# Selection matmuls replaced by VectorE lane shuffles in a fused hash-attention and gated-MLP kernel

## Chip, cores, metric

One core of one Trainium2 chip. The metric is device time in microseconds (us) of one execution of the whole kernel. Times of fast runs are compared with fast runs of the kernel before, taken in the same rounds on the same chip. A ratio is the mean time of one kernel's fast runs over the mean of the other's in the same rounds, so it is not quite the ratio of the medians that are quoted. All runs of this study were in the fast state. Executions of one kernel still spread over 1 to 5 us here, which will matter.

## The reference

Two stages. First, attention in which a query sees only the keys with the same hash: six random projections of each token, taken as sign bits. Then a gated MLP on the heads put side by side.

```python
q_bits = (q @ proj > 0); k_bits = (k @ proj > 0)          # 6 bits a token
mask = bucket(q_bits)[:, :, :, None] == bucket(k_bits)[:, :, None, :]
scores = where(mask, q @ k.T / 8, -1e9)                   # B=4, H=8, S=768, D=64
x = softmax(scores) @ v                                   # -> (3072, 512)
g = x @ w_gate; val = x @ w_val                           # 512 -> 1536
out = x + sigmoid(x @ w_res) * ((gelu(g) * val) @ w_out)  # 1536 -> 512
```

The kernel gets the mask out of the score matmul itself: beside the 64 rows of q and k it has 7 more, six bits as plus or minus a half and one level. A pair of tokens with unequal bits then gets a score so low that its exponential is nothing.

## The kernel before

Two heads make a pair; four batches have four pairs each, 0 to 15. A pair takes nine slots (the first one twelve) of one score chunk each, and a hand-written table says which other work is issued in which slot. The projection of batch b-1 is cut into single matmuls and dealt out into the slots of batch b, by estimated costs, so that TensorE never runs dry. Between two batches stand gate and value matmuls with nothing beside them.

How the bits come about: the hash matmul gives, for four quarters of the tokens (two heads or two pairs, q and k), 32 lanes each on its own 32 partitions; VectorE compares with zero ("hb"). A token's column is there, but four tokens of a stripe are stacked in lanes: lane 6a+i of a quarter is bit i of stripe a. Before the change, four matmuls with a selection table put the stripes side by side:

```python
def hash_half(p, dh, bank=(tp_ps, "tp")):
    ...
        nc.vector.tensor_scalar(hb, hs, 0.0, 0.5, op0=ALU.is_gt, op1=ALU.subtract)
        bits[p] = (hb, bit_pool.tile([P, n, P], BF16, tag="bits", name="bits"))

def spread_matmuls(p, dst, c0, c1):
    for c in range(c0, c1, 4):
        n = min(4, c1 - c)
        for a in range(4):
            nc.tensor.matmul(dst[:, c - c0:c - c0 + n, 32 * a:32 * a + 32],
                             sels[quarters(p)[1]][:, a].rearrange("p j n -> p (j n)"),
                             bits[p][0][:, c:c + n, :], start=True, stop=True)

def spread(p, c0, c1, bank=(tp_ps, "tp")):
    sp = bank[0].tile([P, c1 - c0, P], FP32, tag=bank[1], name="spr")
    spread_matmuls(p, sp, c0, c1)
    nc.vector.tensor_copy(bits[p][1][:, c0:c1, :], sp)      # PSUM -> SBUF

def mask_rows(p, engines=(nc.sync, nc.sync)):               # 7 rows into q's and k's tiles, by DMA
    for h in (1, 0):
        for side in range(2):
            ...
            engines[side].dma_start(mask_target(p, side, h), src[0:NROW])
```

And the table of the later groups, two pairs at a time (s0 is the first slot of pair p-2, so slot 18 is the first of pair p):

```python
for p in range(6, NPAIR, 2):
    ...
    for dh in range(2):
        at(s0 + 7 + dh, hash_half, p, dh)
    for i, s in enumerate((9, 12, 13)):
        at(s0 + s, spread, p, 4 * i, 4 * i + 4)
    at(s0 + 13, mask_rows, p)
    ...
    at(s0 + 10, load, p + 1, (2,))
    if p + 2 < NPAIR:
        at(s0 + 5, load, p + 2, (0, 1))
        at(s0 + 8, load, p + 3, (0, 1))
        at(s0 + 15, load, p + 2, (2,))
```

## Time and profile before

| | before |
|---|---|
| median time | 353.75 us (353.47 to 354.38, 4 runs) |
| span of the profiled run | 352.0 us |
| TensorE busy | 340.3 us, 97% |
| VectorE busy | 152.7 us, 43% |
| selection matmuls | 112, of which 96 are concerned |

In the views, PE is TensorE, PEld its weight loads, DVE VectorE, ACT ScalarE, POOL GpSimd, and SPq the queue in which SyncE issues transfers one after the other. PSUM is the memory that matmuls write to, in banks; "the chain" is the work that ended last, followed back step by step to what released it.

The page, the chain and the matmuls' start times are shown in the prediction. One view more is the backbone of what follows: the stretches between landmarks. I cut the span at the first gate matmul of each batch and at the first projection matmul after it. Here are the four attention stages of the kernel before. Columns: stretch, its length, then busy time and (instructions) of TensorE, its weight loads, VectorE, ScalarE and GpSimd, the granted clock, the share of the DMA engines, GB/s.

```profile
13.00:52.87 39.87, 36.65 (x514) 23.90 (x520) 23.35 (x40) 34.60 (x38) 31.25 (x44) 1.00 0.73 205
85.12:135.99 50.87, 49.84 (x525) 29.10 (x533) 24.77 (x37) 40.54 (x44) 33.78 (x40) 1.00 0.58 158
168.11:218.01 49.90, 49.41 (x524) 28.99 (x532) 22.56 (x34) 40.22 (x43) 31.15 (x36) 1.00 0.41 114
250.30:296.24 45.94, 45.18 (x472) 26.69 (x478) 15.62 (x26) 37.05 (x40) 16.32 (x17) 1.00 0.16 45
```

The second number of each line is the one to compare: how long the stage lasted.

### The profile page before, as it was taken

The numbers are of one execution on the slowest core, as the hardware profiler recorded it, in microseconds if no ns is written. First come the engines' busy times: TensorE is split into PE (matmuls) and PEld (weight loads), VectorE is DVE, ScalarE is ACT, GpSimd is POOL, SyncE is SP. The second block draws the span as 40 slices with busy tenths as digits, with TensorE's granted clock in tenths as the row PEclk, the third lists the DMA queues.
The fourth block names the chain that finished last, engine by engine and source line by source line (L and its number), as shares of the span: only waits on it lengthen the run. The fifth ranks groups of instructions, "written<-read, shape, count | busy, mean of one in ns | idle before, by whom it ended". The sixth has DMA issues, their size and how long they took to land.

```text
span 352.0 us, 7561 instructions
## 1 busy us (share of the span) xinstructions
PE 340.3 (97%) x3056; PEld 202.4 (57%) x3106; DVE 152.7 (43%) x231; ACT 211.3 (60%) x238; POOL 154.0 (44%) x194
## 2 busy tenths in 40 slices
PE   8999889999999999999999999999999999999995
PEld 4656466665565566656465566666555665666443
DVE  6975532435436427343344446333452024433343
ACT  5899895235787886323888788323778884232220
POOL 5798947675488487200068678400038222000000
PEclk9999999999999999999999999999999999999999
DMA  7875879998813882820005663510002221000012
GB/s 222 258 238 108 257 252 299 361 336 176 259 49 93 203 252 69 210 102 0 2 35 128 175 204 105 125 41 1 0 2 63 85 54 50 10 2 1 32 60 89
DMA packets 52718, 44.06 MB, mean 125 GB/s; under 512 B 31656, under 2 KB 44620, under 8 KB 52684
## 3 DMA queue, kind: packets, MB, share of 16 engines
q1 hardware_dynamic: 52540, 43.56, 42.6%
q8 instruction: 24, 0.39, 0.5%
q14 instruction: 10, 0.08, 0.1%
q0 software_dynamic: 64, 0.02, 0.0%
q10 hardware_dynamic: 80, 0.00, 0.0%
HBM read 29.36 MB, written 6.29 MB: 101 GB/s over the span
## 4 chain that ended last, share of the span: by engine, by line
PE 89%; ACT 4%; DVE 4%; issue 2%; DVEq 0%; ACTq 0%
PE sp L457 35%; PE fps L492 16%; PE sp L435 15%; PE av L406 9%; PE rps L477 5%; PE hs L274 4%; ACT e L439 4%; PE spr L287 2%; DVE x_tok L383 1%; PE wps L182 1%; DVE o L498 1%; PE tp L392 1%; DVE total L376 1%; PE tp L217 0%; DVE bits L294 0%
## 5 line engine op out<-in xcount | busy, mean ns | idle before, releaser
L439 ACT ACTIVATE e<-sp 128x1024 bf16<-128x1024 f32 (+1 forms) x147 | 144.3, 1007 | 30.3 <-PE sp L435 25.6
L463 ACT ACTIVATE gt<-sp 128x768 bf16<-128x768 f32 x48 | 39.0, 812 | 82.9 <-PE sp L457 82.9
L464 DVE SCALAR_TENSOR_TENSOR hh<-gt,sp 128x768 bf16<-128x768 bf16 x48 | 45.8, 954 | 80.8 <-PE sp L457 80.8
L492 PE MATMUL fps<-wo,hh 128*128 128x512 bf16 (+2 forms) x284 | 73.1, 369 | 1.3 <-DVE o L498 0.3
L457 PE MATMUL sp<-x_sb,wg 128*128 128x256 bf16 (+1 forms) x378 | 70.4, 325 | 0.3
L457 PE MATMUL sp<-x_sb,wv 128*128 128x512 bf16 (+1 forms) x374 | 69.7, 324 | 0.5
L406 PEld LDWEIGHTS <-e 128*128 128x128 bf16 x1152 | 50.0, 97 | 31.1 <-issue 9.3
L406 PE MATMUL av<-va,e 128*128 128x65 bf16 x1152 | 56.1, 193 | 0.7
L435 PE MATMUL sp<-aug,aug 71*128 71x512 bf16 x192 | 54.3, 326 | 2.4 <-ACT e L439 1.5
L457 PEld LDWEIGHTS <-wv 128*128 128x128 bf16 x384 | 37.6, 98 | 24.8
L457 PEld LDWEIGHTS <-wg 128*128 128x128 bf16 x384 | 37.3, 98 | 24.5
L435 PE MATMUL sp<-second,second 128*128 128x256 bf16 (+1 forms) x175 | 47.8, 320 | 0.2 <-ACT e L439 0.2
L501 POOL TENSOR_TENSOR o<-o,x_tok 128x512 f32<-128x512 f32 x18 | 20.8, 1155 | 57.2 <-DVE o L498 52.5
L492 PEld LDWEIGHTS <-hh 128*128 128x128 bf16 x300 | 28.3, 97 | 25.1
L498 DVE SCALAR_TENSOR_TENSOR o<-th,fps 128x512 f32<-128x512 f32 (+2 forms) x25 | 16.5, 659 | 42.1 <-PE fps L492 37.5
L383 POOL TENSOR_TENSOR x_tok<-total,rec 128x768 bf16<-128x768 f32 x9 | 13.3, 1473 | 47.4 <-DVE rec L382 47.4
L208 POOL COPY second<-aug 64x768 bf16<-64x768 bf16 x30 | 24.4, 825 | 15.6 <-DMA aug<-nat 14.7
L237 DVE STREAM_TRANSPOSE t<-ld 128x768 f32<-128x768 f32 (+1 forms) x34 | 29.6, 905 | 0.5 <-DMA ld<-in_q_dram 0.4
L480 ACT ACTIVATE th<-rps 128x512 f32<-128x512 f32 x24 | 14.3, 596 | 18.3 <-PE rps L477 14.1
L477 PE MATMUL rps<-wr,x_sb 128*128 128x512 bf16 x95 | 24.4, 379 | 0.1
L435 PEld LDWEIGHTS <-second 128*128 128x128 bf16 x192 | 18.5, 97 | 5.1 <-issue 2.2
L435 PEld LDWEIGHTS <-aug 71*128 71x128 bf16 x192 | 16.4, 97 | 5.9 <-issue 1.7
(67 smaller groups left out, 246.0 us busy)
## 6 DMA issues: line engine op xcount, KB each, us to landing
ldv<-in_v_dram SPq DMA_DIRECT2D x16, 384.0 KB
out_dram<-o SPq DMA_DIRECT2D x23, 256.0 KB
ld<-in_q_dram SPq DMA_DIRECT2D x15, 384.0 KB
ld<-in_k_dram SPq DMA_DIRECT2D x15, 384.0 KB
ws<-in_moe_w_gate_dram SPq DMA_DIRECT2D x6, 512.0 KB
ws<-in_moe_w_val_dram SPq DMA_DIRECT2D x6, 512.0 KB
ws<-in_moe_w_out_dram SPq DMA_DIRECT2D x6, 512.0 KB
ws<-in_moe_w_res_dram SPq DMA_DIRECT2D x2, 512.0 KB
```

What stands on the lines that cost most here:

```text
L208: eng.tensor_copy(second[x[0] % NM][x[1]][D:P], aug[x][D:P])
L237: nc.vector.transpose(t32[x][:, c0:c1].rearrange("p c h n -> p (c h n)"), raw[x][:, c0:c1].rearrange("p c d -> p (c d)"))
L406: nc.tensor.matmul(o[:, qt0 + i, :], e[:, off + i * P:off + (i + 1) * P], va[:, hi, jt, 0:D + 1], start=(hi not in begun), stop=(jt == T - ...
L435: nc.tensor.matmul(sp[:, off:off + nq * P], ks[0:n, jt, :], qs[0:n, qt0:qt0 + nq, :], start=True, stop=True)
L439: nc.scalar.activation(e[:, 0:n], sp[:, 0:n], AF.Exp, scale=float(ALPHA))
L457: nc.tensor.matmul(sp[:, c0:c1], w[:, kk, bass.ts(m, P)], xs[:, kk, c0:c1], start=(kk == 0), stop=(kk == KM - 1))
L463: nc.scalar.activation(gt, sp[:, 0:S], AF.Gelu)
L464: nc.vector.scalar_tensor_tensor(hh[:, m, :], gt, 0.5, ps[1][:, 0:S], op0=ALU.mult, op1=ALU.mult)
L477: nc.tensor.matmul(rps, x_sb[b][:, kk, t, :], wr[:, kk, :], start=(kk == 0), stop=(kk == KM - 1))
L492: nc.tensor.matmul(fps, hh[:, m, bass.ts(t, P)], wo[:, m, cs], start=(m == 0), stop=(m == KF - 1))
L498: nc.vector.scalar_tensor_tensor(o[:, cs], th[:, cs], 1.0, fps, op0=ALU.add, op1=ALU.mult)
L501: last.tensor_add(o3, o3, x_tok[b][:, k0:k1, t, :])
```

## The change

The intent: take the 96 selection matmuls off TensorE, which is the bound, and let VectorE, which is not, pick the lanes. The level row, which the selection table made out of the constant halves, comes from a per-partition scalar in the compare. The first pair keeps its matmuls.

```diff
-            nc.vector.tensor_scalar(hb, hs, 0.0, 0.5, op0=ALU.is_gt, op1=ALU.subtract)
-            bits[p] = (hb, bit_pool.tile([P, n, P], BF16, tag="bits", name="bits"))
+            first = isinstance(p, tuple)
+            nc.vector.tensor_scalar(hb, hs, 0.0, 0.5 if first else levels[int(p >= HP)],
+                                    op0=ALU.is_gt, op1=ALU.subtract)
+            bits[p] = (hb, None if first else
+                       bit_pool.tile([P, n, P], BF16, tag="bits", name="bits"))
...
+    def spread(p, a):
+        hb, out = bits[p]
+        lanes = [NBITS * a + i for i in range(NBITS)] + [4 * NBITS] * (32 - NBITS)
+        nc.vector.stream_shuffle(out[:, :, 32 * a:32 * a + 32], hb, lanes)
...
-        for i, s in enumerate((9, 12, 13)):
-            at(s0 + s, spread, p, 4 * i, 4 * i + 4)
+        for a, s in enumerate((9, 10, 12, 13)):
+            at(s0 + s, spread, p, a)
...   (pairs 1 to 4 likewise; make_level in place of the second make_sel; spread no longer
...    costs a slot 0.25 us nor closes it to a new projection row)
```

> **What bounds the kernel now.** I read the busy table first, then the chain of work that ended last, then that chain cut by stage, and only then single instructions in order of time.
>
> ```profile
> span 352.0 us, 7561 instructions
> PE 340.3 (97%) x3056; PEld 202.4 (57%) x3106; DVE 152.7 (43%) x231; ACT 211.3 (60%) x238; POOL 154.0 (44%) x194
> PE 89%; ACT 4%; DVE 4%; issue 2%; DVEq 0%; ACTq 0%
> ```
>
> TensorE is busy 97% of the span and 89% of the chain that sets the end runs over it; VectorE has 57% of its time free. So time taken off TensorE is worth time, and time put on VectorE is worth nothing unless something on the chain waits for it. But the average hides stages, and the next lines, the chain cut to 13-53 us, 85-136 us, 168-217 us and 250-296 us (one line each, in this order), show them.
>
> ```profile
> by line: ACT e L439 26.7%; PE sp L435 23.9%; PE av L406 16.9%; PE hs L274 11.8%; issue 4.9%; DVE x_tok L383 4.8%; PE spr L287 3.1%; PE av L413 2.9%; PE tp L392 1.7%; DVE bits L294 1.5%; DVE rec L382 1.2%; PE tp L217 1.1%; ACTq L439 0.1%
> by line: PE fps L492 26.8%; PE sp L435 25.8%; PE av L406 16.4%; PE rps L477 8.4%; PE hs L274 6.1%; PE spr L287 3.5%; DVE x_tok L383 3.0%; ACT e L439 2.0%; DVE total L376 1.9%; issue 1.5%; DVE bits L294 1.4%; DVE o L498 1.3%; PE tp L392 1.0%
> by line: PE fps L492 29.4%; PE sp L435 29.0%; PE av L406 16.9%; PE rps L477 8.8%; PE hs L274 6.4%; PE spr L287 3.6%; ACT e L439 2.1%; DVE t L237 1.8%; DVE o L498 1.3%; issue 1.1%; PE av L418 0.5%; ACTq L439 0.0%
> by line: PE fps L492 28.7%; PE sp L435 28.2%; PE av L406 17.4%; PE rps L477 11.3%; PE hs L274 3.4%; DVE total L376 2.1%; DVE x_tok L383 2.1%; PE spr L287 2.0%; issue 1.4%; ACT th L480 1.3%; DVE share L374 0.7%; PE av L418 0.5%; DVE rec L382
> ```
>
> "PE spr L287" are the selection matmuls that the change removes. The first batch (13-53 us) is shared between ScalarE's exponentials and TensorE, with no output projection to fill the gaps. In the three later attention stages the projection of the batch before ("fps", "rps") fills every gap, and TensorE is the only bound. The four stretches between them (the gate and value matmuls, and the last projection) hold no selection matmul at all: they can only shift. The chain's share of "spr" is 40 x 3.1% = 1.24 us, 51 x 3.5% = 1.79, 49 x 3.6% = 1.76 and 46 x 2.0% = 0.92: 5.7 us together, a first ceiling.
>
> **What the Trainium skill says.** "TensorE: Matmul & The Clock Gate", section "Wait — 56ns, not 53.3ns?": back-to-back warm matmuls of 128 columns start 55.6 ns apart. The trace agrees: below, four of them at 98.00 are followed by the next group at 98.22, 0.22 us for four. Their printed durations (217 ns) overlap, so 96 x 217 ns would overstate the gain four times. "VectorE: DVE Perf Modes", section "The perf-mode tier table": STREAM_SHUFFLE runs at one element a cycle only, some 2400 ns for 2048 elements. No shuffle is in this trace. Its sister, the 32x32 stream transpose, is: 567 ns for 384 elements and 950 for 768, so 1.0 ns an element and 184 ns fixed, which gives 0.57 us for 384 elements and 0.38 for 192; the page's figure with the same slope gives 0.67 and 0.47 (both are estimates). I take 0.62 and 0.42. "Vector Engine (DVE) Microarchitecture Reference", section 3.8: the lanes to select are loaded by an instruction of their own, there is one set for all four banks, and at 128 partitions a bank stays in its own quadrant. Each of the four shuffles of a group picks other lanes, so each needs its load; I allow 0.06 us for it, guessed from the smallest VectorE instruction here (a memset of 2 columns, 60 ns).
>
> **The change part by part.** A group is pair 1, 2, 3 (192 columns), or the two pairs from 4, 6, ... 14 on (384 columns).
>
> *TensorE loses* 96 of its 112 selection matmuls with their weight loads: 8 in each of three groups, 12 in each of six. The 16 of the first pair stay. Of the 96, 36 stand in the first batch, 24, 24 and 12 in the later stages. What one set of four really holds TensorE, I read from start times:
>
> ```profile
> 97.78 0.38 PE L435 MATMUL sp<-second,second 128*128 128x512 bf16 x1
> 98.00 0.38 PE L287 MATMUL spr<-hb,sel 128*128 128x128 bf16 x4
> 98.22 0.65 PE L406 MATMUL av<-va,e 128*128 128x65 bf16 x16
> ...
> 200.36 0.56 DVE L279 TENSOR_SCALAR hb<-hs 128x384 bf16<-128x384 f32 x1 [4.08 <-PE hs L274]
> 200.69 0.38 PE L435 MATMUL sp<-second,second 128*128 128x512 bf16 x1
> 200.97 0.38 PE L287 MATMUL spr<-hb,sel 128*128 128x128 bf16 x4
> 201.41 0.38 PE L492 MATMUL fps<-wo,hh 128*128 128x512 bf16 x1
> ...
> 261.23 0.38 PE L435 MATMUL sp<-second,second 128*128 128x512 bf16 x1
> 261.86 0.38 PE L287 MATMUL spr<-hb,sel 128*128 128x128 bf16 x4 [0.25 <-ACT th L480]
> 262.08 0.65 PE L406 MATMUL av<-va,e 128*128 128x65 bf16 x16
> ```
>
> A score matmul of 512 columns takes its slot of 0.22 us, so 0.22 after its start the next could run. At 98.00 the set costs 0.22 and nothing else. At 200.97 it came 0.06 late, because the bits (VectorE, 200.36 + 0.56 = 200.92) were not there, and the work behind it started 0.44 later: 0.50 in all. At 261.86 it waited for its PSUM bank, still read by ScalarE: 0.63 in all. I read the fifteen sets of the later stages in this way: nine at 0.22 to 0.27, one at 0.32, four (first sets of a group, waiting for bits) at 0.48 to 0.50, one at 0.63, together 5.0 us, of which 15 x 0.22 = 3.3 us is bare matmul time and 1.7 us is waiting and restarting. The chain's own 1.79 + 1.76 + 0.92 = 4.5 us lies between. **Later stages: 3.3 to 5.0 us off the path.**
>
> *The first batch* must be walked. Pair 1 (16.0 us): eight matmuls, but ScalarE runs without a gap from 15.65 to 19.43, so nothing is won. Pair 2 (22.62 and 23.53): ScalarE is gapless from 21.11 to 26.87; the chain holds 0.12 of it. Pair 3 (28.08): ScalarE idles 0.22 before each exponential here for want of scores; 0.22 won. Pair 4 is best:
>
> ```profile
> 41.97 0.96 DVE L383 TENSOR_TENSOR x_tok<-av,rec 128x768 bf16<-128x768 f32 x1
> 42.84 0.68 DVE L294 CAST bits<-spr 128x512 bf16<-128x512 f32 x1
> 43.57 0.38 PE L287 MATMUL spr<-hb,sel 128*128 128x128 bf16 x4 [0.39 <-DVE bits L294]
> ```
>
> The third set has to wait until VectorE has emptied the bank of the second, and that stands behind the normalisation of the pair before. TensorE's next work starts 0.76 us after it could have, and ScalarE then idles 0.61 for it: 0.6 won.
>
> *VectorE loses* 21 casts of 689 ns and 3 of 417 (14.5 + 1.3 = 15.8 us, and 8.8 us of waiting for selection matmuls at the head of its queue). *It gains* 24 shuffles of 384 columns, 24 x (0.62 + 0.06) = 16.3 us, and 12 of 192, 12 x 0.48 = 5.8 us: 22.1. Net +6 us of 352, to about 45% busy; no bound. But order matters in one place. In the built programs the sequence after pair 1's bits changes from transpose, two casts, transpose to four shuffles, transpose, transpose, and the hash matmuls of pair 2 wait for that last transpose already (an idle of 0.32 at 18.45 in the trace). Bits end at 15.35, four shuffles take 1.9, two transposes 1.9: 19.1 or, at the low estimates and with overlap, 18.8, against 18.23 before. Hash and the scores behind it start 0.3 to 0.7 later, in a spot where ScalarE already idles (0.27 and 0.60): **0.4 lost.** First batch in sum: 0.12 + 0.22 + 0.6 - 0.4 = **0.5 won.**
>
> *GpSimd* loses the second selection table (a memset of 0.53, selects of 0.46 and 2 x 0.22 us, 1.4 us at about 29 us) and gets two tables of levels, a memset and four selects of one column each (5 x 0.1 to 0.2, below 1 us). The first one falls where it idles 1.27 us for the first values to land. The transfers of mask rows are the same, after the last shuffle in the place of the last cast. All nil.
>
> *PSUM:* the spreads leave the two single banks that they shared with the projection; no slot is closed to a new projection row because of a spread. This is inside the 1.7 us above.
>
> Full sum: 3.3 to 5.0 plus 0.5, so 3.8 to 5.5 us; I choose 4.7, near the middle. 353.7 - 4.7 = **349.0 us**.
>
> **Rivals.** (a) *VectorE becomes a wait*: shuffles, unlike the casts, stand in one lump; if one takes 0.9 us or more, the four before the second pair's transposes, and pairs of them ahead of the normalisation that frees the accumulator, hold TensorE. For it: the normalisation is on the chain (L383, 4.8% of the first batch). Against: 57% idle, and in the order of instructions never more than two long shuffles stand before it. It would leave 351 to 352. (b) *Nothing is won in the first batch, and the filling takes the waits back*: the projection is dealt out to slots by estimated costs, which the change lowers by 0.25 us a set, close to what I measured; so the dealing stays sound. Only the bare matmul time would then count: 350.4. (c) *More is won than matmul time*: the chain also shows "DVE bits" at 1.5% and 1.4% (0.6 and 0.7 us). If these were real waits, 5.7 + 1.3 = 7.0 us, 346.7. Against: beside the 0.70 us at 98.42 TensorE ran values and scores throughout, so the chain merely took a side road. (d) *Weights come too late* when the first gate stage starts 0.5 us earlier: the third chunk is cast at 68.97 and needed at about 73.9, so no.
>
> **Range and chances.** The low end is the full reading plus part of (c), the high end (a) in mild form: 347.1 to 351.2 holds it 8 times in 10. 2% is 7.1 us, more than the chain holds of selection matmuls at all, so faster needs (c) entire: 0.06. Slower by 2% needs a new stall of over 11 us: 0.02. Within 2%: 0.92.
>
> **What would show it.** Right: 16 selection matmuls left; TensorE's busy time down by several us with its share still 96 to 97%; shuffles at 0.55 to 0.7 us (384) and 0.38 to 0.5 (192), VectorE near 45%; each later attention stage shorter by 1.4 to 1.9 us (the last by 0.7 to 1.2), the gate stretches unchanged in length; at about 18.5 us a longer wait of the hash matmuls for a transpose; the 0.39 us wait at 43 us gone. Wrong: shuffles near 1 us; new waits of "av" or "hs" matmuls for VectorE; stages that stay as long while TensorE's share falls.

## The result, and the profile after

The changed kernel takes 350.48 us (350.23 to 351.13, 4 runs); ratio 0.9908, 95% interval 0.9889 to 0.9927. That is 3.3 us less, where 4.7 was predicted. First the page's head:

```profile
span 348.5 us, 7427 instructions
PE 335.5 (96%) x2961; PEld 197.0 (57%) x3010; DVE 152.7 (44%) x279; ACT 209.9 (60%) x238; POOL 154.1 (44%) x200
PE 80%; ACT 7%; DVE 4%; POOL 3%; issue 3%; DMA 2%; SPq 1%; DVEq 0%; ACTq 0%; POOLq 0%
```

TensorE lost 4.8 us of busy time, and the span 3.5. VectorE's time is the same to 0.1 us: what the casts cost (15.8 us), the shuffles and their lane loads cost (16.3). The last line is the hint: in the chain that ended last, DMA, the DMA queue (SPq) and GpSimd have turned up, and TensorE has fallen from 89 to 80%. Now the same four stages:

```profile
13.00:51.60 38.60, 35.20 (x478) 22.10 (x482) 23.64 (x63) 34.18 (x38) 30.83 (x44) 1.00 0.71 214
83.85:134.28 50.43, 48.33 (x501) 27.67 (x508) 24.33 (x47) 39.95 (x43) 35.31 (x42) 1.00 0.63 160
166.74:215.66 48.92, 48.38 (x501) 27.54 (x508) 22.73 (x44) 40.05 (x43) 31.06 (x36) 1.00 0.45 116
247.95:292.67 44.72, 44.21 (x461) 25.95 (x467) 15.59 (x31) 36.73 (x40) 16.27 (x17) 1.00 0.19 46
```

Shorter by 1.27, 0.44, 0.98 and 1.22 us. The second stage is the odd one: it lost 24 selection matmuls like the third and gave 0.44. In it the difference of length and TensorE's busy time went from 1.03 to 2.10 us. The order of time in TensorE's row, at the end of that stage, says why:

```profile
127.01 0.40 PE L411 MATMUL av<-va,e 128*128 128x65 bf16 x8
128.63 0.39 PE L440 MATMUL sp<-aug,aug 71*128 71x512 bf16 x1 [1.22 <-DMA aug<-bits]
```

The scores of pair 8, the first of the third batch, wait 1.22 us for the transfer of their mask rows (aug<-bits). Before, the same matmul ran without a wait, 2.85 us after the issue of the last of these transfers (127.14, the second of the pair in the first line):

```profile
126.40 1.42 SPq L323 DMA_DIRECT2D aug<-bits  x2
129.99 0.38 PE L435 MATMUL sp<-aug,aug 71*128 71x512 bf16 x1
```

The chain of this stretch in the changed kernel, with the columns start, length, what:

```profile
120.40 1.02 DVE bits L296 x2
...
121.73 0.46 SPq L90
122.19 0.05 issue
122.24 0.02 SPq L488
122.25 0.03 issue
122.28 0.42 SPq L488
...
122.79 0.75 SPq L328
...
125.08 3.50 DMA aug<-bits
128.63 0.61 PE sp L440 x2
```

The last shuffle ends at 121.42. The queue that issues transfers in order is then still at loads of the next batch (L90) and a store (L488); the four mask-row transfers (L328) follow at 0.75 us each, and the last lands 3.50 us after its issue. So pair 8's rows have a deadline, and the change brought it forward: counted from the stage's start, the scores are due at 43.56 us and no longer at 44.86, while the last row is issued at 41.23 in place of 42.02. That leaves the transfer 2.33 us in place of 2.85. This loss of 0.5 us is the smaller part of the wait. The larger one is that the transfer itself took longer: 3.50 us, where 2.85 had been enough.

The shuffles themselves (form, count, busy time in us, mean of one in ns):

```profile
L296 DVE STREAM_SHUFFLE bits<-hb 128x384 bf16<-128x384 bf16 x24 | 12.3, 550 | 0.0
L296 DVE STREAM_SHUFFLE bits<-hb 128x192 bf16<-128x192 bf16 x12 | 3.5, 350 | 0.0
L296 DVE LOAD_MASK_SELECT bits<-hb x36 | 0.5, 14 | 0.3
```

550 and 350 ns, where 620 and 420 were taken, and 14 ns for a load of lanes where 60 was. The real price is lower still, because they overlap:

```profile
15.37 0.35 DVE L296 STREAM_SHUFFLE bits<-hb 128x192 bf16<-128x192 bf16 x1
15.64 0.01 DVE L296 LOAD_MASK_SELECT bits<-hb  x1
15.64 0.35 DVE L296 STREAM_SHUFFLE bits<-hb 128x192 bf16<-128x192 bf16 x1
```

One starts every 0.27 us, lane load included (0.48 for the long ones, in the same way), against 0.48 and 0.68 in the prediction.

A last difference: the second gate stage is 32.46 us long, 32.12 before. In it VectorE's second multiply starts 0.36 us later after its matmuls than all the others do. I return to this at the end of the experiments.

### The profile page after: what moved, and what is told of

Read it like the earlier page. It is cut to its first block, busy times and chain, and to the rows that moved or that the text cites. A ratio compares the mean times of both kernels' runs of the same rounds, so it can differ in the third digit from the quotient of the medians.

```text
span 348.5 us, 7427 instructions
## 1 busy us (share of the span) xinstructions
PE 335.5 (96%) x2961; PEld 197.0 (57%) x3010; DVE 152.7 (44%) x279; ACT 209.9 (60%) x238; POOL 154.1 (44%) x200
## 3 DMA queue, kind: packets, MB, share of 16 engines
q1 hardware_dynamic: 52540, 43.56, 44.9%
## 4 chain that ended last, share of the span: by engine, by line
PE 80%; ACT 7%; DVE 4%; POOL 3%; issue 3%; DMA 2%; SPq 1%; DVEq 0%; ACTq 0%; POOLq 0%
PE sp L462 35%; PE fps L497 14%; PE sp L440 12%; PE av L411 7%; ACT e L444 6%; PE rps L482 4%; PE hs L281 4%; DVE x_tok L388 1%; PE wps L189 1%; DMA aug<-bits 1%; DVE total L381 1%; DVE o L503 1%; DMA aug<-nat 1%; POOL o L506 1%; SPq L328 1%
## 5 line engine op out<-in xcount | busy, mean ns | idle before, releaser
L462 PE MATMUL sp<-x_sb,wv 128*128 128x256 bf16 (+1 forms) x376 | 69.8, 325 | 0.6 <-DVE hh L469 0.2
L440 PEld LDWEIGHTS <-second 128*128 128x128 bf16 x192 | 18.5, 98 | 6.0 <-issue 3.0
L440 PEld LDWEIGHTS <-aug 71*128 71x128 bf16 x192 | 16.3, 97 | 6.7 <-issue 1.4
```

Source lines behind the costliest of these rows:

```text
L440: nc.tensor.matmul(sp[:, off:off + nq * P], ks[0:n, jt, :], qs[0:n, qt0:qt0 + nq, :], start=True, stop=True)
L462: nc.tensor.matmul(sp[:, c0:c1], w[:, kk, bass.ts(m, P)], xs[:, kk, c0:c1], start=(kk == 0), stop=(kk == KM - 1))
```

## The experiments

My theory: bare matmul time is won as predicted, and part of it is handed to a new wait, the mask rows of the first pair of a batch. Rivals: the missing part was never there (waits counted that were none); the dealing of the projection took it; VectorE took it. Twelve kernels, each timed in five rounds (4 to 6 executions of each are on record). The stage lengths in us, each from the one profile of that kernel, cut at the same landmarks. A profile is of one execution and need not be a typical one: those of first_only and late_only are the slowest of their six, those of the changed kernel and rows_first the fastest of theirs.

| kernel | 1st | 2nd | 3rd | 4th | median us | ratio (95%) |
|---|---|---|---|---|---|---|
| before | 39.87 | 50.87 | 49.90 | 45.94 | 353.75 | 1 |
| after | 38.60 | 50.43 | 48.92 | 44.72 | 350.48 | 0.9908 (0.9889 to 0.9927) |
| first_only | 41.86 | 51.05 | 49.89 | 45.94 | 354.31 | 0.9985 (0.9944 to 1.0026) |
| late_only | 39.93 | 50.96 | 48.65 | 44.71 | 350.47 | 0.9876 (0.9840 to 0.9912) |
| bare_mm | 39.39 | 50.73 | 49.79 | 45.40 | 353.04 | 0.9952 (0.9913 to 0.9991) |
| rows_early | 39.82 | 50.45 | 48.66 | 44.71 | 350.26 | 0.9866 (0.9829 to 0.9902) |
| before_later_set | 40.20 | 50.93 | 50.30 | 46.68 | 355.01 | 1.0025 (1.0007 to 1.0043) |
| rows_first | 38.23 | 49.31 | 48.65 | 44.72 | 349.19 | 0.9862 (0.9840 to 0.9885) |
| rows_both | 39.27 | 49.04 | 48.66 | 44.72 | 349.77 | 0.9884 (0.9864 to 0.9904) |
| shuffle_twice | 43.23 | 50.75 | 48.67 | 45.19 | 354.92 | 1.0030 (1.0009 to 1.0052) |
| after_again | 40.11 | 50.69 | 48.65 | 44.71 | 351.66 | 0.9922 (0.9891 to 0.9953) |
| dealt_as_before | 38.61 | 50.38 | 48.43 | 44.88 | 349.99 | 0.9878 (0.9859 to 0.9898) |
| rows_first_again | 38.30 | 49.05 | 48.65 | 44.72 | 349.03 | 0.9865 (0.9843 to 0.9886) |
| rows_first_v5 | 38.49 | 49.04 | 48.65 | 44.72 | 348.86 | 0.9852 (0.9833 to 0.9870) |

The first four experiments shared their runs of the kernel before (354.55 median), then the next four (353.87), then the last four (354.02). The third and fourth columns repeat to 0.1 us between kernels with the same code there (but for the changed kernel's own first profile, 48.92 in the third stage where the others have 48.65), so a stage length is a far finer ruler than a total. The first column does not repeat, and why is one of the findings.

### The change in halves: first_only, late_only

Selection matmuls and shuffles live side by side in one kernel, chosen by pair:

```diff
+    def shuffled(p):
+        return p <= 4            # first_only;  p > 4 in late_only
```

> Shuffles for pairs 1 to 4 only (the first batch), selection matmuls as before for all later groups. If the stages add up, the first batch gives what it gave in the changed kernel, 1.27 us, and nothing else moves: 352.5 us, ratio 0.9964, first gate matmul at about 51.6 us against 52.87. Rival: the start of the first gate stage is fixed by something else than TensorE's own work (weights, transfers), then the later stages stretch by what the first batch won and the time stays at 353.5 or more.

> Selection matmuls as before for pairs 1 to 4, shuffles for all later groups. If the stages add up: the changed kernel's total of 3.3 us less the first batch's 1.3, so 351.7 us, ratio 0.9943, and the wait of the score matmuls for the mask rows (1.2 us at about 128 us in the changed kernel) is there again. Rival, that this wait comes only because the first batch ended earlier: no such wait, 350.6 us.

The later stages behave as separate parts: first_only leaves the third and fourth at their old lengths, late_only brings them to 48.65 and 44.71. And late_only has the wait for the mask rows at the end of the second stage, though its first stage is as long as before:

```profile
130.02 0.39 PE L461 MATMUL sp<-aug,aug 71*128 71x512 bf16 x1 [1.27 <-DMA aug<-bits]
```

So the wait doesn't need an earlier start. In this kernel the scores were due 3.37 us after the last row's issue, later than before, and still waited: the transfer took 4.59 us. Nor is it wholly the later groups' change: first_only, which has the selection matmuls there, waits 0.39 us at the same place (132.41). The kernel before already stood close to this deadline. The expectation of 351.7 us was above the 350.47 measured (ratio 0.9876 against 0.9943); in single stages nothing explains more than 2 us, so a part of this is the spread of the rounds, whose runs of before reached up to 358 us. first_only is the surprise: no gain in its rounds (0.9985, an interval that holds 1), and in its profile, the slowest of six executions by 1.9 us, a first stage 2 us longer. This profile shows another wait for mask rows, those of pair 4 at the end of the first batch:

```profile
49.96 0.38 PE L461 MATMUL sp<-aug,aug 71*128 71x512 bf16 x1 [1.72 <-DMA aug<-bits]
```

Soon after, the granted clock was half for 3.4 us:

```profile
51.37:54.79 3.42, 3.17 (x27) 2.21 (x26) 1.48 (x2) 2.27 (x4) 2.08 (x2) 0.50 1.03 350
```

With TensorE busy for 3.17 us of it, that is worth some 1.6 us (an estimate, half of the busy time). The wait and the clock together more than undo the stage's gain. In the profile of the changed kernel the wait at this place was 0.27 us, and put down to ScalarE. The first batch's gain is thus a matter of luck from execution to execution; after_again, below, shows the same.

### Bare matmul time: bare_mm

The 96 matmuls come back into the changed kernel, in their old slots, with constant operands and into the bank that the slot's scores overwrite, so that they wait for no bits and no bank of their own.

```diff
         sp = sc_ps.tile([P, 1024], FP32, tag="sp", name="sp")
+        for i in range(dummies.get((p, c), 0)):
+            nc.tensor.matmul(sp[:, P * (i % 4):P * (i % 4) + P], ident, eps_sb,
+                             start=True, stop=True)
```

> The changed kernel plus the 96 matmuls of 128 columns again, in the slots of the old ones, but with constant operands, into the score bank of the slot, read by nobody: the bare TensorE time of the selection without its waits for bits and banks. By the prediction's split bare time is 15 sets x 0.22 = 3.3 us in the later stages and near 0.3 us in the first batch: 350.5 + 3.6 = 354.1 us at most, and still 353 if the wait for mask rows swallows a part. If the waits and restarts that the prediction counted at 1.7 us were real and won, this kernel must come out clearly faster than before, at 352 us; if it comes out at 353.7 or above, only bare matmul time was won.

```profile
167.83:217.62 49.79, 49.79 (x534) 28.97 (x533) 22.48 (x44) 39.80 (x43) 31.14 (x36) 1.00 0.41 114
249.90:295.30 45.40, 45.27 (x480) 26.60 (x479) 15.59 (x31) 36.94 (x40) 16.26 (x17) 1.00 0.18 45
```

Against 48.65 and 44.71 without them, 24 matmuls cost 1.14 us and 12 cost 0.69: 48 and 57 ns each, where 55 was predicted. The bare time is right. The rest, from these lengths to those of the kernel before, is what its waits cost: 50.87 - 50.73, 49.90 - 49.79 and 45.94 - 45.40, that is 0.14 + 0.11 + 0.54 = 0.8 us. The prediction had counted 1.7. This rest also holds the other dealing of the projection, which dealt_as_before, below, puts at up to 0.2 us a stage. The total can't decide between 0.8 and 1.7: 353.04 us, ratio 0.9952 (0.9913 to 0.9991), is 0.3 to 3.1 us below the kernel before, whose runs in these rounds spread over 4.7 us.

### A wait that was none: before_later_set

Where did the other 0.9 us come from? I had read 0.22 us of "restart" behind the first set of four groups. The weight loads of that place in the kernel before tell another story:

```profile
201.13 0.15 PEld L492 LDWEIGHTS <-hh 128*128 128x128 bf16 x2
201.41 0.38 PE L492 MATMUL fps<-wo,hh 128*128 128x512 bf16 x1
```

Two weight loads for projection matmuls, and one matmul. The other one ran in the 0.22 us that looked empty; its record is missing. Over the whole run there are 300 loads of this kind and 284 matmuls:

```profile
L492 PE MATMUL fps<-wo,hh 128*128 128x512 bf16 (+2 forms) x284 | 73.1, 369 | 1.3 <-DVE o L498 0.3
L492 PEld LDWEIGHTS <-hh 128*128 128x128 bf16 x300 | 28.3, 97 | 25.1
```

To test it, the kernel before with its first set one slot later, where bits are long ready:

```diff
-        for i, s in enumerate((9, 12, 13)):
+        for i, s in enumerate((10, 12, 13)):
```

> The kernel before with one edit: the first set of selection matmuls of each later group stands one slot later (10 in place of 9), where its bits are long there. The prediction booked 0.26 us of waiting and restarting on four of these five sets, 1.1 us in sum. If that was a real cost, this kernel is about 1.1 us faster than the kernel before (ratio 0.997). The traces now suggest that 0.22 us of each was a projection matmul whose record is missing (its weight load is there), so that only some 0.05 us a set is waiting: then 0.2 us, which is within the noise of the timing, and the stage lengths in the trace (50.87, 49.90, 45.94 us) move by 0.1 each at most.

It is no faster; 355.01 us, ratio 1.0025, a little slower. The second stage tests it best: two of the five moved sets stand there, no wait for mask rows disturbs it, and it is 50.93 us long, 50.87 before. The restart was no cost. That the kernel became slower is a miss of mine in sign: the third stage grew by 0.4 and the fourth by 0.7 us. The profile shows a wait for mask rows of 0.69 us in the fourth (at 270.04) and one of 0.53 in the first, which the edit does not touch; the third stage's growth I did not trace.

### Is the deadline the cause: rows_early, rows_first, rows_both

Three ways to have the rows there in time. First, shuffles and rows in earlier slots:

```diff
-        for a, s in enumerate((9, 10, 12, 13)):
+        for a, s in enumerate((9, 9, 10, 10)):
-        at(s0 + 13, mask_rows, p)
+        at(s0 + 11, mask_rows, p)
```

> The changed kernel with the four shuffles of each later group in slots 9, 9, 10, 10 in place of 9, 10, 12, 13 and the transfers of its first pair's mask rows in slot 11 in place of 13. If the 1.2 us wait for the mask rows at 128 us is what keeps the second batch from its predicted gain, it goes and the time falls by about 1.2 us, to 349.3 us (ratio 0.9874). Rival: the wait is hidden in slack that closes elsewhere, or the earlier transfers collide with the transposing ones, then 350.5 us as before the edit; rival that VectorE in one lump of four shuffles holds back the normalisation: slower than 350.5.

```profile
123.40 0.53 SPq L90 DMA_DIRECT2D ldv<-in_v_dram  x1
124.02 1.50 SPq L328 DMA_DIRECT2D second<-bits  x2
125.62 1.48 SPq L328 DMA_DIRECT2D aug<-bits  x2
```

And in TensorE's row, the first scores that need them:

```profile
129.75 0.39 PE L440 MATMUL sp<-aug,aug 71*128 71x512 bf16 x1 [0.84 <-DMA aug<-bits]
```

The second stage stayed at 50.45. Though the rows stand two slots earlier in the program, they were issued at 124.02, no earlier (122.79 in the changed kernel, whose first stage was 1.22 us shorter): the queue was busy until then with transposing transfers and loads that stand before them. The scores again began near 129.7, after a wait of 0.84 us. The bits were not late; the queue was. So, second, leave the shuffles and put loads behind the rows:

```diff
-            at(s0 + 8, load, p + 3, (0, 1))
+            at(s0 + 14, load, p + 3, (0, 1))
-        at(s0 + 10, load, p + 1, (2,))
+        at(s0 + 14, load, p + 1, (2,))
```

> The changed kernel with only transfers reordered: the loads of the next pair's q and k, and of the odd pair's v, stand in slot 14, behind the mask rows of slot 13, in place of 8 and 10. If the 1.2 us wait of the score matmuls at the batch boundary near 128 us comes from the mask rows having to queue behind those loads, it goes: second attention stage about 49.3 us in place of 50.43, the total 1.2 us lower than the changed kernel (349.3 us, ratio 0.9874). Rival, that the rows land late whatever stands before them (the four issues take 3 us and the landing 2.3): wait stays at 0.5 us or more. Rival, that the loads then come too late for casts and hashes of the next pairs: new waits for transfers, no gain.

```profile
83.48:132.79 49.31, 48.91 (x510) 27.73 (x508) 24.43 (x47) 39.96 (x44) 32.88 (x39) 1.00 0.58 158
```

49.31 us as expected, and 349.19 us in all. The scores of pair 8 begin almost on time, as the last row lands:

```profile
123.47 1.42 SPq L328 DMA_DIRECT2D aug<-bits  x2
127.05 0.39 PE L440 MATMUL sp<-aug,aug 71*128 71x512 bf16 x1
```

What this stage had not given stood behind 1.2 MB of loads (three of 384 KB). "DMA: Bandwidth & Descriptors" of the Trainium skill says, under "Two DMAs through the same engine are not ordered", that within one queue of one DMA engine descriptors start in order. The trace agrees as far as it goes: wherever the scores of pair 8 waited clearly, the three loads stood before the rows, and the last row took 3.1 to 4.6 us from issue to landing (seven profiles); with the loads behind it, 2.8 us here (124.20 to 127.05). The kernel before has the loads in front as well, but there 1.2 us pass between the issue ahead of the rows (a store, until 123.61) and theirs (124.85); in the changed kernel 0.1. Counted from the stage's start the last row is issued only 0.5 us earlier than in the changed kernel, so the larger part of the gain is the faster landing. What the loads do to it, by their place in the queue or by sharing the DMA engines, no run separates.

Third, the same for pair 4, whose rows are late in some executions: all four shuffles in its first slot, rows in the next.

```diff
-        at(base(3) + a, spread, 4, a)
-    at(base(3) + 3, mask_rows, 4)
+        at(base(3), spread, 4, a)
+    at(base(3) + 1, mask_rows, 4)
```

> As the previous, and for pair 4 the four shuffles stand together in its first slot, so that its mask rows are issued about 1.2 us earlier, ahead of the first batch's end, where some executions show a wait for these rows of 0.3 to 1.7 us at 49 us. If this wait sets the end of the first batch, that stage measures about 38.5 us every time (39.87 before) and the total falls another 0.3 to 1 us. Rival: the two shuffles that now stand ahead of the normalisation of pair 2 (0.95 us) hold back the value matmuls by as much, and nothing is won or 0.5 us is lost.

The rival had it: value matmuls waited 0.58 us at 43.20 for the normalisation behind the shuffles, and the rows were still 0.26 us late. This execution also waited 1.9 us in the second gate stage (34.51 us long) for x's transposing transfer, which now stands behind the loads that were moved:

```profile
PE sp L462 <- DMA x_sb<-x_tok: 1.9, 1, 1.9
```

rows_first did not show this in its first profile, but 1.5 us of it in its second, and rows_first_v5 shows 0.8. No kernel without the moved loads shows it. The wait has partly moved from mask rows to this transfer. On average rows_first still wins, as the direct comparison below shows.

### Is VectorE free: shuffle_twice

```diff
-        nc.vector.stream_shuffle(out[:, :, 32 * a:32 * a + 32], hb, lanes)
+        for _ in range(2):
+            nc.vector.stream_shuffle(out[:, :, 32 * a:32 * a + 32], hb, lanes)
```

> The changed kernel with every shuffle done twice: 36 more shuffles, 12 x 0.27 + 24 x 0.475 = 14.6 us more of VectorE. If VectorE's time is free except through the deadline of the mask rows, each group's rows come 1 to 1.9 us later and the time rises by what the two tight boundaries (first batch and second) show of that: 1 to 2.5 us, all as waits for mask rows, none in the third and fourth attention stage. Rival, that VectorE is a bound in its own right: 4 us or more, spread over all stages. Rival, free altogether: under 0.5 us.

```profile
13.00:56.23 43.23, 37.43 (x480) 22.69 (x478) 29.52 (x94) 34.02 (x37) 30.84 (x45) 0.96 0.64 193
171.35:220.02 48.67, 48.67 (x510) 27.48 (x509) 26.57 (x61) 39.79 (x43) 30.78 (x36) 1.00 0.45 117
```

The total rose by some 4 us, more than my 1 to 2.5, and as much as the rival had said, but not spread over all stages. In the third stage 4 us more of VectorE cost nothing: 48.67 against 48.65. The fourth grew by 0.5 us, 0.3 of it a new wait for mask rows. In the first stage 6 us more cost 3 to 5 us, by all three ways: hash matmuls waiting for transposes (1.1 us over the run), value matmuls for the normalisation (1.1), scores for mask rows (1.9), and a clock of 0.96 (half for 3.4 us). So VectorE's time is free in the third stage, nearly so in the fourth, and not free in the first one. My expectation underrated how near that stage is to its limits on every engine.

### Dealing, and the kernel again: after_again, dealt_as_before, rows_first_again, rows_first_v5

One call, the same rounds. after_again is the changed kernel unedited, rows_first_again the kernel above. dealt_as_before deals the projection out as if the selection matmuls still stood there:

```diff
+        for x in sl:                     # the old slots of the selection matmuls
+            uses_tp.add(x)
+            busy[x] += 0.25
```

> The changed kernel unedited, for a second profile and for times in the same rounds as the next kernels: ratio 0.991 as on record (0.989 to 0.993). First attention stage between 38.2 and 39.9 us, depending on how long the scores of pair 4 wait for their mask rows near 49 us; second stage 50.4 with the wait for mask rows at its end, third 48.7 to 48.9, fourth 44.7.

> The changed kernel, but the projection matmuls are dealt out to the slots as if the selection matmuls still stood there (their 0.25 us a set added to the slot's cost, their slots closed to a new projection row). If dealing is a side matter, as the prediction's second rival was answered, the time is that of the changed kernel within 0.5 us. Rival: the new dealing is what brings the scores of the next batch forward into the wait for the mask rows; then the wait is shorter here and the time 0.5 to 1 us lower, or the dealing is worth a part of the gain and the time is 1 us higher.

The second profile of the changed kernel has both waits in full:

```profile
49.44 0.38 PE L440 MATMUL sp<-aug,aug 71*128 71x512 bf16 x1 [1.54 <-DMA aug<-bits]
130.41 0.38 PE L440 MATMUL sp<-aug,aug 71*128 71x512 bf16 x1 [1.49 <-DMA aug<-bits]
```

Its first stage is 40.11 us, 1.5 longer than in the first profile: the whole first-batch gain gone with one late transfer. This run of rounds gave 351.66 us, 0.9922; my upper limit of 39.9 us for the stage was too low. Its two slowest executions (352.51 and 352.95) have a mean granted clock of 0.995 and 0.993 where the rest have 0.998 to 1; one stretch of 3.4 us at half clock in some 350 is 0.005. Without them the mean is 350.7. With the old dealing the wait at the second boundary was 0.54 us and the total 349.99; its interval just overlaps that of after_again, which holds the two executions at a lower clock, so whether the dealing moved the deadline is not settled. Third and fourth stage differ by 0.2 us each way: dealing did not take the gain.

rows_first_v5 also moves one load behind pair 4's rows:

```diff
-    at(base(2) + 6, load, 5, (2,))
+    at(base(3) + 4, load, 5, (2,))
```

> The kernel with the loads behind the mask rows, unedited, in the same rounds as the changed kernel: 1.3 us below it (ratio to before 0.987 where the changed kernel has 0.991), second stage 49.3 us.

> As the previous, and the load of pair 5's values stands behind the mask rows of pair 4 too (slot 4 of pair 3 in place of slot 6 of pair 2), 0.38 MB less in front of them. If the wait for pair 4's rows at 49 us is made by transfers queued before them, it shrinks and the first stage stays at 38.2 to 38.6 us in every execution: median 0.3 us lower than the previous kernel and less spread. Rival: the weights (2 MB) in front of it make the wait, and nothing changes.

rows_first_again has 0.9865 (0.9843 to 0.9886) where the changed kernel in the same rounds has 0.9922 (0.9891 to 0.9953): the intervals do not meet, and the medians are 2.6 us apart. About half of this is the changed kernel's two executions at a lower clock: without them the means are 350.7 and 349.3, which is the 1.3 us that I expected. (The lower clock may itself follow from a late row, as in first_only; these two were not profiled.) rows_first_v5 has the lowest ratio of all, 0.9852, and the narrowest spread (348.45 to 349.30, 4 runs), but it is not clearly different from rows_first_again. Both had a first stage without the wait for rows (38.30 and 38.49), so the load moved last is not shown to matter. Both beat the kernel before and the changed one.

What stays open: the 0.35 us in the second gate stage. Of fourteen profiles, those of before, before_later_set and shuffle_twice have 32.12 us there; where nothing else waits the other kernels have 32.46 to 32.48. VectorE then starts one multiply 0.36 us late although its matmuls are done: the second of the stage in most kernels, the seventh in first_only, the eleventh in late_only. Counted in the packed traces, with the sequencer's records, it is VectorE's 192nd instruction in all eleven, and a transfer of the queue "q14 instruction" starts 0.7 to 1.3 us after it begins. In the three kernels without the delay the 192nd falls into an attention stage (at 178.58 us in the kernel before). So the 0.35 us goes with how many instructions VectorE has had by then, and the change gives it more (393 records in place of 349). That VectorE waits there for its next instructions to be fetched is a guess; no run tests it.

## Why the prediction was right, and where it was not

The time, 350.48, lies in the range, and "within 2%" was right. By steps:

- *TensorE is the bound, and bare matmul time counts.* Right. Predicted 3.3 us in the later stages; bare_mm measured 1.14 and 0.69 us in the third and fourth, where 1.32 and 0.66 were predicted.
- *"1.7 us is waiting and restarting".* Mis-sized: 0.8 us measured (before less bare_mm, give or take the dealing). Four readings of 0.22 us were a projection matmul without a record. The choice of a point near the middle of 3.3 to 5.0 hid this: 3.3 + 0.8 = 4.1, and rows_first, which in its profile has next to nothing of the new wait, shortened the three stages by 1.56 + 1.25 + 1.22 = 4.0 us.
- *First batch, 0.5 won.* Mis-sized, in the term "0.4 lost": the hash of pair 2 was to start 0.3 to 0.7 us late behind the shuffles. ScalarE's idle time at that spot rose from 0.27 to 0.36 us only, since four shuffles take 1.1 us and not 1.9. The other terms came: the idle of 0.61 at pair 4 gone, 0.22 at pair 3 gone, and 0.60 at pair 2 down to 0.39. Without a late row, the stage gave 1.3 to 1.6 us.
- *"The transfers of mask rows are the same ... All nil."* This is the step that failed. The transfers are the same, but the scores that need them came 1.30 us sooner, the rows were issued only 0.8 us sooner, and, close behind the loads, they took 3.5 us to land where 2.85 had been enough. The wait costs 1.2 to 1.5 us in the second stage of the changed kernel and 0 to 1.5 in the first. It is a new wait in the place of those removed; I had looked for one on VectorE and not in the DMA queue. That the third and fourth stage show nothing of it goes with lighter DMA use there (0.45 and 0.19 of the engines' time against 0.63), and in the third with more time: there the rows had 3.71 us from the last issue to the first use, against 2.33.
- *VectorE near 45%, shuffles 0.55 to 0.7 and 0.38 to 0.5 us.* 44%, 0.55 and 0.35: at or just under the low end. The estimates of 0.67 and 0.47 from the page's figure are not "with the same slope": they take one element a cycle, 1.04 ns, and the transpose's 1.0 would have given 0.74 and 0.54. *A longer wait of the hash matmuls near 18.5 us*: not seen. *The 0.39 us wait at 43 us gone*: yes. *Each later stage shorter by 1.4 to 1.9 us, the last by 0.7 to 1.2*: 0.44 and 0.98 in the second and third, both short of it (1.25 in the third in most other profiles), and 1.22 in the last. *Gate stretches unchanged*: the second grew by 0.34. The second stage, shorter by 0.44 us while TensorE's busy time in it fell by 1.5, comes close to the sign named for being wrong.
- *Rival (a), VectorE in the way*: not in this kernel, though shuffle_twice shows that the first batch has little room. *Rival (b)* was the nearest in the total, for another reason: 350.4 was its number, but the waits were won, and lost to the rows. *Rival (c)*, more than matmul time: no.

Sum of what was measured: 4.0 (later stages) + 1.3 (first stage), less 1.2 to 1.5 for pair 8's rows, 0 to 1.5 for pair 4's, 0.35 in the gate stage: 2 to 3.8 us, which holds both measurements of the changed kernel (3.3 and 2.4). That the time fell into the range is in part luck: the first batch gave about 0.8 us more than was booked for it, and this made up for more than half of a wait that was not booked at all.

## What to carry to other kernels

When work is taken off the bounding engine, everything that it consumes is due earlier: list for each stage boundary what must have landed, and how long before its use it did; a transfer that lands just in time is the next bound. Small urgent transfers belong in front of large patient ones in the same queue, and here that order was worth some 2 us in the mean (0.9865 against 0.9922 of 354 us), 1.3 without the changed kernel's two executions at a lower clock; the change by itself gained 2.8 in the same rounds. Read the time from issue to landing as well as the time of issue: here the landing moved more. Before a gap in TensorE's row is counted as a wait, compare matmuls with weight loads there: a gap of just one matmul's length may be one whose record is missing.

## What the Trainium skill lacked or had wrong

- "VectorE: DVE Perf Modes", "The perf-mode tier table", has one size for STREAM_SHUFFLE (some 2400 ns at 2048 elements). Here 384 elements took 550 ns and 192 took 350: 1.04 ns an element, which agrees with one element a cycle, and 150 ns fixed; back to back they start every 0.48 and 0.27 us. A fixed part got from the page's figure (270 ns) was too high. Section 5.2 of the page named next does have a slope and a fixed part for built-in instructions of one source; it doesn't name the shuffle, and the prediction didn't use it.
- "Vector Engine (DVE) Microarchitecture Reference", section 3.8, names the load of the lane selection but no time for it: 14 ns here, hidden in the 0.27 us from one shuffle to the next.
- No page read gives the price of a per-partition scalar in place of a constant: the same compare out of PSUM took 618 ns in place of 558 (384 columns), and 417 in place of 357 (192).
- "TensorE: Matmul & The Clock Gate" speaks of an idle window of some 3.4 us before the clock falls. Here the clock fell to half for 3.4 us (51.37 to 54.79 in first_only) after a stretch of the same length in which TensorE was busy for 1.69 us and waited 1.72 in one piece; waits of 1.54 and 1.49 us were not followed by any fall.
- "Perfetto Trace Analysis" advises weight-load time over matmul time as a measure; it does not say that matmul records can be missing. Here 300 weight loads of the projection stand against 284 matmuls.
